# Scores computed in four column tiles, and an order that keeps to one tiling of TensorE

## The chip, the core and the metric

The kernel runs on one core of a Trainium2 chip, as one program in one launch. The metric is the device time of one execution in microseconds (us); lower is better. The times given are medians over several executions. Of the engines, TensorE (PE; its weight loads are shown apart as PEld) does the matrix products, ScalarE (ACT) the exponentials, VectorE (DVE) and GpSimd (POOL) the elementwise work, and SyncE (SP) issues most transfers.

## The reference

Two rounds of two layers, each added to a residual stream of 2048 tokens by 512 features. Layer A is full attention with 32 query heads of 16 features and one head of keys and values. Layer B is attention within four segments of 512 tokens, with a memory that grows from segment to segment. Everything is float32.

```python
def _A_ref(x, wq, wk, wv, wo):
    q = (x @ wq) as [32 heads, 2048, 16];  k = x @ wk;  v = x @ wv
    p = softmax(q @ k.T * 16 ** -0.5)
    return (p @ v, heads side by side) @ wo

def _B_ref(x, wq, wk, wv, wo, beta):          # per head, L = 512
    for s in range(4):
        qs, ks, vs = q[s], k[s], v[s]
        p = softmax(qs @ ks.T * scale + causal mask of the segment)
        a_mem = (phi(qs) @ M) / (phi(qs) @ z + 1e-6)
        o = g * a_mem + (1 - g) * (p @ vs)
        M, z = M + phi(ks).T @ vs, z + sum(phi(ks))
    return o @ wo

x = x + _A_ref(layernorm(x), ...);  x = x + _B_ref(layernorm(x), ...)     # twice
```

## The kernel before

**Two streams.** Work is cut into four blocks of 512 tokens and, for the two rounds, into eight phases f. In phase f the full attention of one block of queries (stream `za`, generator `a_units`) is woven with everything that follows from the block before (stream `zb`, generator `side`): output projection, layer norm, the whole of layer B for that block, its output projection, and the projections that the next full attention needs. Phase 0 weaves the first full attention with the preparation of all keys; after phase 7 the last block's `side` runs alone. Each generator yields, ahead of each piece of work, a function that tells when the piece is ready by the kernel's own account of the engines (`clk`). `weave` takes the next piece from the stream that is ready, and where both are, in proportion to their lengths; `par` does the same among the chains inside one stream. What they choose is the program order, and a scheduler keeps to that on PE apart from small moves. PE runs its instructions in that order.

**A stage of the full attention.** One stage is one tile of 128 keys for 4 heads by 512 queries; there are 1024. It has two score steps (L600), each of two matmuls into a pair of PSUM banks: stationary `kst`, 97 rows (the six products of bfloat16 parts, and a guard row) by 128 keys; moving `qa`, 97 by 512. After each step ACT takes the exponential of the pair, 128 x 1024 (L603), into `pa`. Then `a_pv` multiplies with the values: four float32 matmuls, one for each head, with stationary `va` of 17 columns (16 values and a one for the sum). Each writes 17 partitions of the bank `pva`, from partition 64, 96, 0 and 32, so it occupies 32 columns of the array. `together` records them; the first stands at L77, the other three at L80. A float32 matmul is one instruction in the program's order and two matmul records in the profile, for the two parts of its weights.

**The segment attention.** For each of the 64 units (4 heads of one block) `b_rowmax` computes all scores once for the row maxima (L771; stationary `qb`, moving `kb`, 128 to 512 columns), which DVE reduces (L779). `b_attend` computes them again, transposed (L807), adds the causal mask on the diagonal as a product of the identity `idb` with `maskk` (L810), ACT takes the exponential (L814) and `b_pv` multiplies with the values as `a_pv` does (into `pvb`, with `pb` and `vb`).

**The projections** (`project`, L341) are float32r matmuls at the array's full width, 12 to a result of 128 x 512: four contraction tiles with three products of parts each. They yield after every three. Transposes (L401, L738), the memory (L832, L868) and small products with 32 columns or fewer (L467, L552) are the rest of PE's work.

Of the kernel before, what the change touches and what calls it, by code (L numbers as in the profile page):

```python
# [33 lines left out]
P = 128  # L34
# [33 lines left out]
def net_kernel(ctx, tc, x_in, a_wq, a_wk, a_wv, a_wo, b_wq, b_wk, b_wv, b_wo, b_beta, cst, out):  # L68
# [3 lines left out]
    T = nc.tensor  # L72

    def together(first, *a, **k):
        """a matmul; all but the first of a group follow the one before at once"""
        if first:
            nc.tensor.matmul(*a, **k)  # L77
        else:
            with tc.high_priority(offset=400):
                tc.keep_in_program_order(nc.tensor.matmul(*a, **k))  # L80

# [21 lines left out]
    HOP = 250.0  # from one engine's end to the start of what waits for it on another  # L103
    LOAD = 2600.0  # a small transfer
    clk = {"pe": 0.0, "act": 0.0, "dve": 0.0, "pool": 0.0}
    evac_on = ["dve"]

    def pe(cost):
        clk["pe"] += cost
        return clk["pe"]  # L110
# [41 lines left out]
    # static tiles  # L152
# [32 lines left out]
    def wload(kind, i, w=None, parts=""):  # L185
        """into w, else into the next of the ring; parts: keep the two parts, or take those kept"""
# [56 lines left out]
    # gate of the memory, one value per partition of the (4 heads x 32) layout, column (p, t)  # L243
# [14 lines left out]
    class Ring:  # L258
        """slots of PSUM, taken in turn"""
# [16 lines left out]
    def layout(kind):  # L276
        """banks: scores, row maxima, the rest; 6 and 7 hold the products with the values"""
# [9 lines left out]

    def par(*gens):
        """several chains at once: the first that is ready, else the one that is ready soonest"""
        live = []  # L290
        for g in gens:
            if g is not None:
                try:
                    live.append([g, next(g)])
                except StopIteration:
                    pass
        while live:
            yield lambda: min(z[1]() for z in live)
            now = clk["pe"]
            z = next((z for z in live if z[1]() <= now), None) or min(live, key=lambda z: z[1]())  # L300
# [29 lines left out]
    xr = [0.0] * 4  # when each quarter of xh, xl is there  # L330

    def project(out_, lhs_h, lhs_l, rhs_h, rhs_l, need):
        """out_ = sum over 4 contraction tiles of (h + l)(h + l), without l*l; takes a slot of the ring"""
# [5 lines left out]
        for kt in range(4):  # L339
# [3 lines left out]
            end = pe(648)  # L343
            if kt < 3:
# [5 lines left out]
    def project_t(w):  # L350
        """transposed: [128 columns of w, 512 tokens]"""
# [3 lines left out]
    def slot(shape, need):  # L355
        """a slot of the ring for a short piece of work"""
# [13 lines left out]
    def norm_stats(xt, tiles, t0):  # L370
        """mean and 1/sqrt(var + eps) of token tiles xt (their numbers: tiles), there at t0"""
# [41 lines left out]
    def evac(ps, e):  # L413
        """one reader of a PSUM slot; the rest goes on from SBUF"""
# [7 lines left out]
    def split3(x, t):  # L422
        """three bfloat16 parts that add up to x, there at t"""
# [627 lines left out]
```

## Time and profile before

| | |
|---|---|
| median of 3 runs | 3380.35 us (3379.74 to 3380.38) |
| profiled execution | span 3373.7 us from the first to the last instruction, 6.6 us around it: 3380.3 us |
| busy share of the span | PE 98%, ACT 71%, DVE 49%, PEld 37%, POOL 11% |
| chain that ended last | PE 80%, issue 8%, DVE 5%, DMA 4% |
| score matmuls of the full attention, L600 | 4096, mean 381 ns |
| exponentials of the full attention, L603 | 2048, mean 1022 ns |
| value products, L77 and L80, full attention | 2048 and 6144 records, mean 598 ns |
| granted TensorE clock | 0.990 |

A record's length holds the way through the array, so matmuls that stream one behind the other overlap in the profile; how fast they run is read from the distance between starts. "Issue" in the chain is time in which an engine waited for nothing that the profile shows. Idle time of an engine that is not the bottleneck costs nothing.

### The profile page before, as it was taken

How to read it: one execution, taken by the hardware profiler on the slowest of the kernel's cores; microseconds unless marked ns; L12 is line 12 of the kernel's file. 1: busy time of each engine (PE TensorE's matmuls, PEld its weight loads, DVE VectorE, ACT ScalarE, POOL GpSimd, SP SyncE). 2: the span in 40 equal slices, each digit the busy share in tenths (PEclk: the TensorE clock that was granted, in tenths of full speed). 3: DMA queues.
4: the chain of work that ended last, by engine and by line, in shares of the span. 5: the costliest groups of instructions: out<-in, count | busy, mean ns of one | idle time of the engine just before them, and what ended most of it. 6: DMA issues, size and time to landing. Idle time of an engine off the chain costs nothing.

```text
span 3373.7 us, 53649 instructions
## 1 busy us (share of the span) xinstructions
PE 3289.8 (98%) x20586; PEld 1252.0 (37%) x20586; DVE 1644.6 (49%) x4679; ACT 2404.7 (71%) x2575; POOL 377.6 (11%) x540
## 2 busy tenths in 40 slices
PE   7999999999999999999999999999999999999977
PEld 4422333334333443334433333333433334333533
DVE  7701345454553545645455353555455534553466
ACT  3699777866778667786678878677677776778422
POOL 2100110021100220102110020100110002100100
PEclk9999999999999999999999999999999999999978
DMA  4411121122210231202322142321231215221341
GB/s 133 130 33 29 56 84 56 33 78 85 69 54 20 72 91 56 72 15 82 101 64 75 45 123 78 111 61 52 79 85 50 58 39 161 90 65 29 124 121 42
DMA packets 188674, 244.62 MB, mean 73 GB/s; under 512 B 26904, under 2 KB 147576, under 8 KB 188408
## 3 DMA queue, kind: packets, MB, share of 16 engines
q1 hardware_dynamic: 169272, 176.08, 17.7%
q0 software_dynamic: 19136, 65.02, 6.8%
q8 instruction: 164, 2.69, 0.4%
q14 instruction: 102, 0.84, 0.1%
HBM read 168.41 MB, written 72.61 MB: 71 GB/s over the span
## 4 chain that ended last, share of the span: by engine, by line
PE 80%; issue 8%; DVE 5%; DMA 4%; POOL 2%; ACT 1%; SPq 0%; DVEq 0%; POOLq 0%; ACTq 0%
PE bank L77 28%; PE bank L600 24%; PE bank L341 13%; PE bank L771 4%; PE bank L807 4%; PE bank L810 1%; PE bank L80 1%; DMA sb<-parts 1%; PE bank L832 1%; DVE mo L779 1%; DMA wst<-in_B_wq_dram 1%; PE bank L401 1%; POOL w L120 1%; PE bank L868 1%; ACT pa L603 1%
## 5 line engine op out<-in xcount | busy, mean ns | idle before, releaser
L603 ACT ACTIVATE pa<-bank 128x1024 f32<-128x1024 f32 x2048 | 2010.1, 1022 | 610.9 <-PE bank L600 597.2
L600 PE MATMUL bank<-qa,kst 97*128 97x512 bf16 x4096 | 1147.4, 381 | 3.1 <-ACT pa L603 1.8
L80 PE MATMUL bank<-pa,va 128*17 128x512 f32 x6144 | 1072.0, 598 | 0.0
L77 PE MATMUL bank<-pa,va 128*17 128x512 f32 x2048 | 1057.5, 598 | 2.9 <-DVE t L632 1.9
L779 DVE CUSTOM_DVE_ANT_0 mo<-bank,maskq 128x512 bf16<-128x512 f32 (+3 forms) x1024 | 498.7, 487 | 572.7 <-PE bank L771 557.8
L600 PEld LDWEIGHTS <-kst 97*128 97x128 bf16 x4096 | 313.8, 97 | 796.2 <-issue 640.0
L814 ACT ACTIVATE pb<-bank 128x1024 f32<-128x1024 f32 (+2 forms) x384 | 331.6, 881 | 179.8 <-PE bank L810 143.1
L341 PE MATMUL bank<-xh,w 128*128 128x512 f32 x832 | 322.1, 432 | 6.1 <-DVE qmx L471 2.7
L771 PE MATMUL bank<-kb,qb 96*128 96x512 bf16 (+3 forms) x1024 | 251.7, 309 | 26.4 <-DVE m L779 22.9
L341 PE MATMUL bank<-w,xh 128*128 128x512 f32 x752 | 269.8, 437 | 4.7 <-DVE xh L665 2.1
L77 PEld LDWEIGHTS bank<-pa,va 128*17 128x17 f32 x2048 | 117.5, 95 | 406.8 <-issue 325.2
L120 POOL TENSOR_SCALAR w<-wst 128x512 fp32r<-128x512 f32 x160 | 103.8, 649 | 1272.6 <-PE bank L341 1202.0
L807 PE MATMUL bank<-qb,kb 98*128 98x512 bf16 (+3 forms) x1024 | 222.9, 305 | 4.1 <-ACT pb L814 2.8
L632 DVE STREAM_TRANSPOSE t<-bank 128x512 f32<-128x512 f32 x88 | 62.8, 714 | 298.3 <-PE bank L80 297.9
L771 PEld LDWEIGHTS <-qb 96*128 96x128 bf16 x1024 | 87.2, 99 | 302.4 <-issue 247.2
L341 PEld LDWEIGHTS bank<-xh,w 128*128 128x128 f32 x832 | 158.4, 191 | 86.5 <-issue 32.7
L80 PE MATMUL bank<-pb,vb 128*17 128x512 f32 (+3 forms) x1536 | 186.0, 439 | 0.0
L77 PE MATMUL bank<-pb,vb 128*17 128x512 f32 (+3 forms) x512 | 182.6, 439 | 1.0 <-ACT pb L814 0.4
L341 PEld LDWEIGHTS bank<-w,xh 128*128 128x128 f32 x752 | 135.0, 189 | 109.5 <-issue 45.1
L341 PE MATMUL bank<-xl,w 128*128 128x512 f32 x416 | 166.5, 400 | 1.2 <-DVE xl L409 1.2
L208 DVE TENSOR_TENSOR w<-wst,w 128x512 fp32r<-128x512 f32 x160 | 112.0, 700 | 101.0 <-POOL w L120 100.2
L341 PE MATMUL bank<-w,xl 128*128 128x512 f32 x376 | 150.7, 402 | 0.0
(136 smaller groups left out, 2480.5 us busy)
## 6 DMA issues: line engine op xcount, KB each, us to landing
sb<-parts SPq DMA_DIRECT2D x192, 128.0 KB
qa<-sd SPq DMA_DIRECT2D x88, 196.0 KB
sd<-parts SPq DMA_DIRECT2D x96, 128.0 KB
x<-xt SPq DMA_DIRECT2D x48, 256.0 KB
xt<-x SPq DMA_DIRECT2D x48, 256.0 KB
qb<-sb SPq DMA_DIRECT2D x64, 192.0 KB
kb<-sb SPq DMA_DIRECT2D x64, 192.0 KB
qa<-sd SPq DMA_DIRECT2D x88, 128.0 KB
```

The lines of the kernel that those rows point to most:

```text
L77: nc.tensor.matmul(*a, **k)
L80: tc.keep_in_program_order(nc.tensor.matmul(*a, **k))
L120: G.tensor_scalar(o, i, 1.0, 0.0, op0=ALU.mult, op1=ALU.add)
L208: V.tensor_tensor(w[:, 1, :], s, f(w[:, 0, :]), op=ALU.subtract)
L341: T.matmul(ps, lhsT=l_(kt), rhs=r_(kt), start=n == 0, stop=n == 11)
L600: T.matmul(sc[:, i, :], lhsT=L["kst"][0:rows, kt * P:(kt + 1) * P], rhs=q[0:rows, 2 * u + i, :], start=True, stop=True)
L603: A.activation(x, sc, AF.Exp, scale=0.25)
L632: V.transpose(t1.rearrange("p a b -> p (a b)"), pva)
L771: T.matmul(ps[:, o_:o_ + nk], lhsT=q[0:96, j, qt * P:(qt + 1) * P], rhs=k[0:96, j, 0:nk], start=True, stop=True)
L779: V.tensor_tensor_reduce(out=mo[:, 0:nk], in0=ps[:, o_:o_ + nk], in1=maskq[:, 512 - nk:512], op0=ALU.add, op1=ALU.max, scale=1.0, scalar=- ...
L807: T.matmul(sc[:, i, o_:o_ + nq], lhsT=k[0:98, 2 * u + i, kt * P:(kt + 1) * P], rhs=q[0:98, 2 * u + i, kt * P:512], start=True, stop=False)
L814: A.activation(e[:, :, 0:w], sc[:, :, 0:w], AF.Exp, scale=0.25)
```

## The change

Three things change. The constants of PE's account are edited along with them.

**Scores in four column tiles.** `by_columns` replaces each score matmul and each mask matmul. It takes 32 of the 128 stationary columns at a time, in the order 2, 3, 0, 1, and writes 32 partitions of the same PSUM bank: four weight loads and four matmuls where there was one of each, with the same moving operand. This holds for L600, L771, L807 and L810. No result changes.

**An order that knows the tiling.** A yield may carry its form: `Need(at, "cols")` for the scores and value products, "full" for all else. `tiling` keeps the form of the last work, and a change of form is accounted 95 ns. `par` prefers among the ready chains one whose form is at hand. `weave` compares scores: the time at which a stream could start, 190 ns more if the form changes, and 0.03 of the stream's lead over its share.

**Projections in halves.** They yield once, after six matmuls, and no longer after every three.

```diff
+    def by_columns(first, out_, lhsT, rhs, **k):
+        for c in (2, 3, 0, 1):
+            r_ = slice(32 * c, 32 * c + 32)
+            together(first and c == 2, out_[r_], lhsT=lhsT[:, r_], rhs=rhs, **k)
...
-    def pe(cost):
-        clk["pe"] += cost
+    tiling = ["full"]
+    def pe(cost, form="full"):
+        clk["pe"] += cost + (DRAIN if form != tiling[0] else 0.0)
+        tiling[0] = form
         return clk["pe"]
...
+        def pick():
+            ready = [z for z in live if z[1]() <= clk["pe"]]
+            same = [z for z in ready if form_of(z[1]) == tiling[0]]
+            return (same or ready or [min(live, key=lambda z: z[1]())])[0]
...
-            if ra <= now and rb <= now:
-                use = za if da / ta <= db / tb else zb
-            else:
-                use = za if ra <= rb else zb
+            lag = (da / ta - db / tb) * (ta + tb) / 2
+            def score(z, r, ahead):
+                return max(now, r) + (2 * DRAIN if form_of(z[1]) != tiling[0] else 0.0) + LAG * ahead
+            use = za if za[1] and score(za, ra, lag) <= score(zb, rb, -lag) else zb
...
-            end = pe(648)
-            if kt < 3:
+            end = pe(660)
+            if kt == 1:
                 yield lambda: 0.0
...
-                        T.matmul(sc[:, i, :], lhsT=L["kst"][0:rows, kt * P:(kt + 1) * P],
-                                 rhs=q[0:rows, 2 * u + i, :], start=True, stop=True)
+                        by_columns(i == 0, sc[:, i, :], L["kst"][0:rows, kt * P:(kt + 1) * P],
+                                   q[0:rows, 2 * u + i, :], start=True, stop=True)
...
-                T.matmul(ps[:, o_:o_ + nk], lhsT=q[0:96, j, qt * P:(qt + 1) * P], rhs=k[0:96, j, 0:nk],
-                         start=True, stop=True)
+                by_columns(o_ == 0, ps[:, o_:o_ + nk], q[0:96, j, qt * P:(qt + 1) * P], k[0:96, j, 0:nk],
+                           start=True, stop=True)
...
-                        T.matmul(sc[:, i, o_:o_ + P], lhsT=idb, rhs=maskk, start=False, stop=True)
+                        by_columns(False, sc[:, i, o_:o_ + P], idb, maskk, start=False, stop=True)
```

The account also changes: a value product of the full attention from 940 to 848, one of the segment attention loses 85, a triple of a projection goes from 648 to 660. In the changed kernel the first matmul of a group stands at L81, the others at L84, whatever they compute; projections stand at L378.

What that does to PE's order is seen at three places. First, a stage of the full attention with nothing beside it, before (names as in the profile, with numbers; a row is one instruction, or several alike):

```order
L77 MATMUL bank<-pa_2058,va_16_106 17x512
L80 MATMUL bank<-pa_2058,va_16_106 17x512
L80 MATMUL bank<-pa_2054,va_16_106 17x512 x2
L600 LDWEIGHTS kst_14_104
L600 MATMUL bank<-qa_18_112,kst_14_104 128x512
L600 LDWEIGHTS kst_14_104
L600 MATMUL bank<-qa_18_112,kst_14_104 128x512
```

and the same place on PE now, the last matmul of one stage's scores, its value products, and the start of the first group of the next scores:

```order
L84 MATMUL bank<-qa_19_113,kst_14_104 32x512
L81 MATMUL bank<-pa_3210,va_16_106 17x512
L84 MATMUL bank<-pa_3210,va_16_106 17x512
L84 MATMUL bank<-pa_3200,va_16_106 17x512 x2
L81 LDWEIGHTS kst_14_104
L81 MATMUL bank<-qa_19_113,kst_14_104 32x512
L84 LDWEIGHTS kst_14_104
L84 MATMUL bank<-qa_19_113,kst_14_104 32x512
```

Scores that took one load and one matmul of 128 columns now take four of 32, and everything in the stage has outputs of at most 32 partitions.

Second, a projection of layer B (weights `w`, tokens `xh` and `xl`) woven into the full attention on PE, before:

```order
L600 MATMUL bank<-qa_18_112,kst_14_104 128x512
L341 MATMUL bank<-w_2815,xh_139 128x512 x2
L341 MATMUL bank<-w_2815,xl_140 128x512
L600 LDWEIGHTS kst_14_104
L600 MATMUL bank<-qa_18_112,kst_14_104 128x512
L600 LDWEIGHTS kst_14_104
L600 MATMUL bank<-qa_18_112,kst_14_104 128x512
L77 MATMUL bank<-pa_3399,va_16_106 17x512
L80 MATMUL bank<-pa_3399,va_16_106 17x512
L80 MATMUL bank<-pa_3382,va_16_106 17x512 x2
L341 MATMUL bank<-w_2820,xh_139 128x512 x2
L341 MATMUL bank<-w_2820,xl_140 128x512
```

and such a projection on PE now:

```order
L84 MATMUL bank<-qa_19_113,kst_14_104 32x512
L378 MATMUL bank<-w_7584,xh_139 128x512 x2
L378 MATMUL bank<-w_7584,xl_140 128x512
L378 MATMUL bank<-w_7613,xh_139 128x512 x2
L378 MATMUL bank<-w_7613,xl_140 128x512
L378 MATMUL bank<-w_9708,xh_139 128x512 x2
L378 MATMUL bank<-w_9708,xl_140 128x512
L378 MATMUL bank<-w_9713,xh_139 128x512 x2
L378 MATMUL bank<-w_9713,xl_140 128x512
L81 LDWEIGHTS kst_14_104
L81 MATMUL bank<-qa_19_113,kst_14_104 32x512
```

The pieces of three that stood between scores are now twelve in a row. Runs of exactly twelve were 64 before and are 153 now.

Third, the segment attention on PE, a score step with its mask, before:

```order
L807 MATMUL bank<-qb_21_115,kb_24_118 128x512
L807 LDWEIGHTS kb_24_118
L807 MATMUL bank<-qb_21_115,kb_24_118 128x512
L810 LDWEIGHTS idb_94
L810 MATMUL bank<-maskk_96,idb_94 128x128
```

and one of its shortest steps now, from the end of its scores to the start of its masks:

```order
L84 MATMUL bank<-qb_20_114,kb_23_117 32x128
L84 LDWEIGHTS kb_23_117
L84 MATMUL bank<-qb_20_114,kb_23_117 32x128
L84 LDWEIGHTS idb_94
L84 MATMUL bank<-maskk_96,idb_94 32x128
```

Eight instructions of 128 columns stand where two stood. Over the part of the order that is executed, PE has 22,529 instructions before and 65,537 now, 7168 groups of scores and masks both times; neighbours of different form (outputs over 32 partitions, and at most 32) number 2557 before and 709 now; projections are entered 432 times before, 143 of them from work of at most 32 partitions, and 197 times now, 187 of them so. With the full attention alone there stand runs of 97 and 35 stages before, 103 and 32 now. The other engines are given the same work.

More of the change, by code (lines that the diff above doesn't have):

```diff
@@ L104, in net_kernel @@
     LOAD = 2600.0
+    LAG = 0.03
+    DRAIN = 95.0
     clk = {"pe": 0.0, "act": 0.0, "dve": 0.0, "pool": 0.0}
     evac_on = ["dve"]
-    def pe(cost):
-        clk["pe"] += cost
+    tiling = ["full"]
+    def pe(cost, form="full"):
+        clk["pe"] += cost + (DRAIN if form != tiling[0] else 0.0)
+        tiling[0] = form
         return clk["pe"]
@@ L286, in drive, with __init__, __call__, form @@
             clk["pe"] = max(clk["pe"], rdy())
+    class Need:
+        def __init__(self, at, form):
+            self.at, self.form_ = at, form
+        def __call__(self):
+            return self.at()
+        def form(self):
+            return self.form_() if callable(self.form_) else self.form_
+    def form_of(need):
+        return need.form() if isinstance(need, Need) else "full"
     def par(*gens):
@@ L296, in par @@
                     pass
+        def pick():
+            ready = [z for z in live if z[1]() <= clk["pe"]]
+            same = [z for z in ready if form_of(z[1]) == tiling[0]]
+            return (same or ready or [min(live, key=lambda z: z[1]())])[0]
         while live:
-            yield lambda: min(z[1]() for z in live)
-            now = clk["pe"]
-            z = next((z for z in live if z[1]() <= now), None) or min(live, key=lambda z: z[1]())
+            yield Need(lambda: min(z[1]() for z in live), lambda: form_of(pick()[1]))
+            z = pick()
             try:
@@ L582, in a_units @@
             if pend is not None and (gate(f, n, k1) or nxt is None):
-                yield lambda: max(pend[-1], pva_free[0] if pend[1] else 0.0)
+                yield Need(lambda: max(pend[-1], pva_free[0] if pend[1] else 0.0), "cols")
                 a_pv(*pend)
@@ L595, in a_units @@
                 for u in range(2):
-                    yield lambda: max(need, rings["sc"].ready(), L["kr"][kt // 4], gate(f, n, k1))
+                    yield Need(lambda: max(need, rings["sc"].ready(), L["kr"][kt // 4], gate(f, n, k1)), "cols")
                     ring = rings["sc"]
@@ L599, in a_units @@
                     for i in range(2):
-                        T.matmul(sc[:, i, :], lhsT=L["kst"][0:rows, kt * P:(kt + 1) * P],
-                                 rhs=q[0:rows, 2 * u + i, :], start=True, stop=True)
+                        by_columns(i == 0, sc[:, i, :], L["kst"][0:rows, kt * P:(kt + 1) * P],
+                                   q[0:rows, 2 * u + i, :], start=True, stop=True)
                     x = tmp(4, [P, 2, 512], F32, "pa")
                     A.activation(x, sc, AF.Exp, scale=0.25)
-                    ring.free[k] = on("act", pe(432), 904)
+                    ring.free[k] = on("act", pe(432, "cols"), 904)
                     pe_.append(x)
@@ L612, in a_units @@
                 if pend is not None:
-                    yield lambda: max(pend[-1], pva_free[0] if pend[1] else 0.0)
+                    yield Need(lambda: max(pend[-1], pva_free[0] if pend[1] else 0.0), "cols")
                     a_pv(*pend)
                 pend = (L, kt == k0, kt, pe_, (f, b, n, k0, k1), kt == k1 - 1, max(te))
-        yield lambda: max(pend[-1], pva_free[0] if pend[1] else 0.0)
+        yield Need(lambda: max(pend[-1], pva_free[0] if pend[1] else 0.0), "cols")
         a_pv(*pend)
@@ L627, in a_pv @@
                      start=first, stop=last)
-        e = pe(940)
+        e = pe(848, "cols")
         if not last:
@@ L764, in b_rowmax @@
         for job in jobs:
-            yield lambda: max(need, rings["m"].ready())
+            yield Need(lambda: max(need, rings["m"].ready()), "cols")
             ring = rings["m"]
@@ L770, in b_rowmax @@
                 nk = (qt + 1) * P
-                T.matmul(ps[:, o_:o_ + nk], lhsT=q[0:96, j, qt * P:(qt + 1) * P], rhs=k[0:96, j, 0:nk],
-                         start=True, stop=True)
+                by_columns(o_ == 0, ps[:, o_:o_ + nk], q[0:96, j, qt * P:(qt + 1) * P], k[0:96, j, 0:nk],
+                           start=True, stop=True)
                 o_ += nk
-                e = pe(cols(nk))
+                e = pe(cols(nk), "cols")
             o_ = 0
@@ L798, in b_attend @@
             for s_ in range(1 if kt >= 2 else 2):
-                yield lambda: max(gr[n], rings["sc"].ready())
+                yield Need(lambda: max(gr[n], rings["sc"].ready()), "cols")
                 ring = rings["sc"]
@@ L806, in b_attend @@
                     for i in range(2):
-                        T.matmul(sc[:, i, o_:o_ + nq], lhsT=k[0:98, 2 * u + i, kt * P:(kt + 1) * P],
-                                 rhs=q[0:98, 2 * u + i, kt * P:512], start=True, stop=False)
+                        by_columns(i == 0, sc[:, i, o_:o_ + nq], k[0:98, 2 * u + i, kt * P:(kt + 1) * P],
+                                   q[0:98, 2 * u + i, kt * P:512], start=True, stop=False)
                     for i in range(2):
-                        T.matmul(sc[:, i, o_:o_ + P], lhsT=idb, rhs=maskk, start=False, stop=True)
-                    e_ = pe(2 * cols(nq) + 115)
+                        by_columns(False, sc[:, i, o_:o_ + P], idb, maskk, start=False, stop=True)
+                    e_ = pe(2 * cols(nq) + 115, "cols")
                 w = loc[1][1] + nq
@@ L818, in b_attend @@
             if pend is not None:
-                yield lambda: max(pend[4], v_r[0], pvb_free[0] if pend[0] == 0 else 0.0)
+                yield Need(lambda: max(pend[4], v_r[0], pvb_free[0] if pend[0] == 0 else 0.0), "cols")
                 b_pv(t, p, *pend)
             pend = (kt, nq, es, loc, te)
-        yield lambda: pend[4]
+        yield Need(lambda: pend[4], "cols")
         b_pv(t, p, *pend)
@@ L860, in b_pv @@
                      rhs=es[s_][:, i, o_:o_ + nq], start=kt == 0, stop=kt == 3)
-        pe(nq * 4 / 2.4 + 85)
+        pe(nq * 4 / 2.4, "cols")
     def b_memory(b, t, r):
```

## The prediction

> **What bounds the kernel now.** I read the page's first and fourth parts first: which engine is full, and what the chain that ended last is made of.
>
> ```profile
> PE 3289.8 (98%) x20586; PEld 1252.0 (37%) x20586; DVE 1644.6 (49%) x4679; ACT 2404.7 (71%) x2575; POOL 377.6 (11%) x540
> ...
> PE 80%; issue 8%; DVE 5%; DMA 4%; POOL 2%; ACT 1%; SPq 0%; DVEq 0%; POOLq 0%; ACTq 0%
> ```
>
> PE is full and the chain runs through it. The second entry matters here: for 8% of the span, 270 us, the chain waits for nothing that the profile shows. Next the stretches, since an average hides stages (columns: window, busy us and count of PE, PEld, DVE, ACT, POOL, clock, DMA).
>
> ```profile
> 200.00:300.00 100.00, 100.00 (x618) 22.78 (x615) 10.16 (x20) 98.86 (x103) 1.22 (x2) 1.00 0.10 27
> 1000.00:1100.00 100.00, 99.76 (x722) 34.08 (x721) 44.37 (x153) 81.38 (x88) 1.23 (x2) 1.00 0.09 25
> 3200.00:3300.00 100.00, 76.87 (x443) 39.15 (x442) 70.84 (x244) 27.69 (x36) 8.71 (x14) 0.83 0.42 120
> ```
>
> At 200 to 300 us the full attention runs alone, with PE and ACT both full. At 1000 us two streams are woven, PE is full and ACT has a fifth to spare; most of the span is so. After about 3170 us the last block stands alone and PE has holes. The timeline then shows what a busy PE does in one stage of the full attention (start, length, engine, line):
>
> ```profile
> 251.81 0.60 PE L77 MATMUL bank<-pa,va 128*17 128x512 f32 x1
> ...
> 251.82 0.62 PE L80 MATMUL bank<-pa,va 128*17 128x512 f32 x3
> 251.82 0.10 PEld L77 LDWEIGHTS bank<-pa,va 128*17 128x17 f32 x1
> 251.83 0.11 PEld L80 LDWEIGHTS bank<-pa,va 128*17 128x17 f32 x4
> 252.25 0.59 PE L77 MATMUL bank<-pa,va 128*17 128x512 f32 x1
> ...
> 252.80 1.04 PE L600 MATMUL bank<-qa,kst 97*128 97x512 bf16 x4
> ...
> 253.76 0.60 PE L77 MATMUL bank<-pa,va 128*17 128x512 f32 x1
> ```
>
> Four value products of 17 columns start within 0.01 us of each other, each in its own 32 columns of the array, and their second halves follow after 0.44 us: four run in the time of one. From the last halves to the first scores it is 0.55, that is 0.11 more; from four scores (0.22 each) to the next value product it is 0.96 in place of 0.88, that is 0.08 more. Each change between full width and 32-column tiles costs about 0.10 us in which nothing starts. PE's order holds 2557 such changes: 2557 x 0.10 = 256 us, against the chain's 270.
>
> **The change, part by part.** The baseline is the profiled span, 3373.7 us, and 6.6 us around it: 3380.3, at the median (3380.35).
>
> *Changes of tiling.* In the new order I count 709, so 1848 fall away: 1848 x 0.10 = **-185 us** (the chain's 8%, read as 7.5 to 8.5, gives 0.099 to 0.112 each, so -183 to -207).
>
> *Not gained where ACT is full.* Runs of 97 and 35 stages have nothing beside them; now they are 103 and 32. There a stage takes 253.76 - 251.81 = 1.95 us. ACT cannot follow below two exponentials:
>
> ```profile
> 48.84 3.75 ACT L603 ACTIVATE pa<-bank 128x1024 f32<-128x1024 f32 x4
> ```
>
> Four end 3.75 after the first starts, one takes 1.02, so they start every 0.91: a stage cannot go under 1.82. It can win 0.13, not 0.20: 132 x 0.07 = **+9**. The 38 changes saved after the last full-attention stage lie beside PE's holes: **+4**.
>
> *Projections.* They are now given out in halves and stand mostly whole between tiled work. Entered from tiles, the first three matmuls take longer:
>
> ```profile
> 1110.85 0.74 PE L341 MATMUL bank<-w,xh 128*128 128x512 f32 x2
> 1111.42 0.39 PE L341 MATMUL bank<-w,xl 128*128 128x512 f32 x1
> 1111.65 0.63 PE L341 MATMUL bank<-w,xh 128*128 128x512 f32 x2
> 1112.12 0.40 PE L341 MATMUL bank<-w,xl 128*128 128x512 f32 x1
> ```
>
> 0.57 to the third matmul, against 0.47 in the next three: the first weights are not loaded ahead. The order has 143 such entries before and 187 after: 44 x 0.10 = **+5**. Entries from full-width work fall from 289 to 10; I count nothing for them.
>
> *The scores in four tiles.* These are the groups that become four loads and four matmuls each (L771 and L807 have three more forms of 256 each, of 256, 384 and 512 columns):
>
> ```profile
> L600 PE MATMUL bank<-qa,kst 97*128 97x512 bf16 x4096 | 1147.4, 381 | 3.1 <-ACT pa L603 1.8 <-ACT pb L814 0.8 <-DVE qmx L471 0.3
> ...
> L810 PE MATMUL bank<-maskk,idb 128*128 128x128 bf16 x1024 | 140.7, 220 | 0.0
> ...
> L771 PE MATMUL bank<-kb,qb 96*128 96x128 bf16 x256 | 57.2, 223 | 0.0
> ...
> L807 PE MATMUL bank<-qb,kb 98*128 98x128 bf16 x256 | 32.7, 220 | 0.0
> ```
>
> 4096 + 1024 + 1024 + 1024 = 7168 groups; 3 x 7168 = 21,504 more matmuls and as many more loads. No row shows four bf16 tiles at once, so I bound the price of a group. Below: nothing, since the value products stream as fast as one, and their second loads (251.82, 251.83) stand while the first halves run until 252.25, so loads hide behind matmuls in the same columns. Above: 0.10, the projection's unhidden load of 128 columns. The value products are nearest; I take 2 ns of stagger, 7168 x 0.002 = **+14** (0 to 717).
>
> The Trainium skill, "TensorE: Matmul & The Clock Gate", section "The mechanism", says that a weight load overlaps a running matmul only if it goes to another row group. All four tiles use the same rows, so by that rule every load would be paid and the sum would take the 717. The trace does not agree: the second loads stand 0.42 us before the halves that use them, in the same rows.
>
> *Groups of 128 columns* (1024 + 256 + 256 = 1536) stream for only 0.05 us with four loads each. Below nothing, above 0.05 for a load of 128 two-byte columns (half the projection's 0.10): 0 to 77; I take 7 ns, **+10**.
>
> *Issue.* A group needs 8 instructions in place of 2. The quickest rows are these:
>
> ```profile
> 1323.70 0.28 PE L807 MATMUL bank<-qb,kb 98*128 98x128 bf16 x2
> 1323.82 0.28 PE L810 MATMUL bank<-maskk,idb 128*128 128x128 bf16 x2
> 1323.93 0.28 PE L807 MATMUL bank<-qb,kb 98*128 98x128 bf16 x2
> 1324.05 0.28 PE L810 MATMUL bank<-maskk,idb 128*128 128x128 bf16 x2
> ```
>
> Two pairs of load and matmul start every 0.115 us, 28.5 ns an instruction, and that may be streaming alone. At that rate a stage of the full attention, 36 instructions, needs 1.03 us and hides in its 1.7 us. A segment-attention group needs 8 x 28.5 = 228 ns against about 57, 112, 164 and 216 of streaming: 1536 x 0.171 + 512 x (0.116 + 0.064 + 0.012) = 361 us if nothing hides it. Nothing is the lower end: value products and projections beside it bring few instructions and long streams. I take **+10**.
>
> *Waits.* The softmax, evacuations and transfers are unchanged in number. PE is given its score, attention and value work in longer runs of one tiling, and projections go past it. A projection of 12 matmuls holds back the scores queued behind it for some 2.8 us (four times the 0.70 from 1111.42 to 1112.12), and ACT waits for those. ACT's spare fifth covers it; without that, each of the 1024 - 132 = 892 woven stages could fall to ACT's floor, 892 x 0.07 = 62. I take **+5** (0 to 62).
>
> Sum: 3380 - 185 + 9 + 4 + 5 + 14 + 10 + 10 + 5 = 3252 us.
>
> **The rivals.**
>
> *Slower: issue becomes the bound.* If the segment attention's score groups issue at 28.5 ns an instruction and nothing hides it, the sum without the 24 us for stagger and issue is 3228, and 361 make 3589. It turns slower once more than 152 of the 361 (42%) stay unhidden; midway between, 3485. For it: no stretch of this trace asks for that pace beyond a few groups. Against: after an idle wait for a transfer, a load, its matmul and the next load start within 0.03 us, some 15 ns apart:
>
> ```profile
> 2861.58 0.10 PEld L771 LDWEIGHTS <-qb 96*128 96x128 bf16 x1 [1.45 <-DMA qb<-sb]
> 2861.61 0.38 PE L771 MATMUL bank<-kb,qb 96*128 96x512 bf16 x1 [0.56 <-DMA qb<-sb]
> 2861.61 0.31 PEld L600 LDWEIGHTS <-kst 97*128 97x128 bf16 x2
> ```
>
> And the mean asks for less: the order has 22,529 instructions on PE that run, 7168 x 6 = 43,008 come in, and 65,537 in 3250 us are 50 ns each. Chance 0.11.
>
> The Trainium skill, "TensorE: Matmul & The Clock Gate", section "Back-to-back issue gap", gives some 81 ns as the sustained pace of a load and a 128-column matmul. By that the eight would take 324 ns, and this rival would be likelier; the four rows above, 57 ns a pair, do not agree, though they are short.
>
> *Slower: loads are not hidden in tiles.* By half the projection's price, 0.05 a group, 7168 x 0.05 = 358, so 3238 + 358 = 3596; it decides from 142 / 7168 = 20 ns a group. Only an unhidden load speaks for it, and the early second loads against. Chance 0.06.
>
> By the rule of the Trainium skill on row groups, above, the time would end here or beyond; the trace so far disagrees, by the same second loads.
>
> *A smaller gain: waits take it.* PE falls to ACT's floor also where the streams are woven: 3252 + 57 = 3309, and more if the next block's chain of transfers is late too. That chain has room: the last block, alone, takes about 200 us after 3170, a woven one near 400. Chance 0.12, nearly all still faster.
>
> *No change:* only if the tiles of the scores and of the value products do not count as one tiling, and 0.10 stays with each. Chance 0.03.
>
> **How the numbers follow.** The forecast, PE's saved changes less small prices, has 0.68: 3252, with 3200 to 3300 as its own range. Its low end has all four unknown prices at zero (3213) and a change at 0.107. The whole range goes up to 3350, through waits and an issue price of a third of 361; the two slower rivals, 0.17, lie above it. So 3200 to 3350. About 0.2%, 7 us, is what a measurement of this kernel can tell from none: faster 0.80, within it 0.03, slower 0.17.
>
> **What would show it.** PE and PEld: 42,090 records each. The chain's "issue" falls from 8% to 2 or 3%. In a stage, value products follow scores after about 0.22 us, with no hole; four tiles of a score start within some 0.06 us, and a group comes every 0.22. ACT in 200 to 300 us goes up to 108 or 110 exponentials. If groups come every 0.25 or more, loads are paid; if only the segment attention's groups stretch to 0.2 and more at 128 columns, it is issue; if PE shows new idle time ended by ACT, it is the floor.

## The result and the profile after

| | before | after |
|---|---|---|
| median of 4 runs each, same chip | 3380.05 us | 3321.27 us (3319.36 to 3324.97) |
| ratio, 95% interval | | 0.9831 (0.9817 to 0.9845) |
| span of the profiled execution | 3373.7 us | 3323.1 us |

It is faster by 59 us; 128 were forecast. The time lies within the range, far from 3252.

The page of the changed kernel, engines and chain:

```profile
PE 3168.7 (95%) x42090; PEld 1540.5 (46%) x42090; DVE 1650.5 (50%) x4679; ACT 2378.1 (72%) x2575; POOL 383.3 (12%) x540
...
PE 7%; issue 2%; ACT 1%; DVE 1%; DMA 1%; SPq 0%; POOL 0%; DVEq 0%; ACTq 0%; POOLq 0%
```

The count of records is the one forecast. PE was busy for 98% and is for 95%. The chain is followed back over a small part of the span only here, so its 2% of "issue" proves nothing. Two windows of the woven part, in the columns of the prediction:

```profile
1000.00:1100.00 100.00, 96.94 (x1594) 45.91 (x1591) 39.69 (x130) 83.53 (x90) 1.25 (x2) 1.00 0.07 18
1500.00:1600.00 100.00, 96.73 (x925) 46.93 (x917) 54.63 (x115) 62.32 (x68) 21.21 (x28) 1.00 0.26 76
```

Where PE was full to 99.76 in the first of them, 3 us in 100 are now empty, and ACT is still idle for a sixth of the time in one and over a third in the other. The exponentials, the first matmul of each score step, and the first row-max products (busy, mean ns, then the idle time ahead and what ended it):

```profile
L640 ACT ACTIVATE pa<-bank 128x1024 f32<-128x1024 f32 x2048 | 1985.9, 1030 | 521.0 <-PE bank L84 511.0 <-ACT pa L640 0.2
...
L81 PE MATMUL bank<-qa,kst 97*32 97x512 bf16 x2048 | 779.4, 381 | 42.3 <-ACT pa L640 21.8 <-ACT pb L851 10.9 <-DMA qa<-sd 1.8
...
L81 PE MATMUL bank<-kb,qb 96*32 96x512 bf16 (+2 forms) x640 | 217.5, 342 | 30.1 <-DVE m L816 25.8 <-DMA sb<-parts 1.5 <-DVE mrr L592 0.4
```

Ahead of the scores stood 3.1 us of idle time before; now 42.3, of which ACT ended 32.7. Ahead of the row-max products little more shows than before:

```profile
L771 PE MATMUL bank<-kb,qb 96*128 96x512 bf16 (+3 forms) x1024 | 251.7, 309 | 26.4 <-DVE m L779 22.9
```

That is only what shows: a matmul's record lasts 0.38 us, its stream 0.21, so a wait of under 0.17 us lies hidden under the end of the record ahead.

**An account of PE's time.** To see all of it I summed over PE's records the distance between the starts of neighbouring groups (four column tiles that start within 0.06 us are one group), less the streaming of the first (0.417 ns a column, which gives 0.213 us for 512; twice that for the float32 value products). What is left is a gap. At a change of form up to 95 ns of it (into tiles) or 118 (out of them) is called the change; elsewhere up to 25 ns is called small; all above is a wait, put down to the engine whose semaphore the group waits on. The sum and some 20 us at the start make the span. All in us:

| kernel | span | changes | cost of changes | small gaps | waits | of these for ACT, DVE | streaming |
|---|---|---|---|---|---|---|---|
| before | 3373.7 | 2557 | 262 | 63 | 179 | 35, 57 | 2849 |
| after | 3323.1 | 709 | 70 | 95 | 283 | 125, 91 | 2852 |
| column tiles alone (tiles) | 3356.6 | 1097 | 111 | 91 | 280 | 118, 70 | 2854 |
| order alone (order) | 3384.4 | 2591 | 264 | 75 | 172 | 48, 59 | 2850 |
| no charge for a change in the weave (nopref) | 3340.9 | 869 | 87 | 91 | 286 | 125, 81 | 2854 |
| before, cheaper exponentials | 3368.2 | 2555 | 262 | 67 | 167 | 23, 58 | 2848 |
| after, cheaper exponentials | 3265.3 | 705 | 68 | 81 | 234 | 71, 104 | 2858 |
| before, both cuts | 3359.2 | 2549 | 262 | 67 | 158 | 20, 50 | 2848 |
| after, both cuts | 3244.3 | 703 | 68 | 80 | 212 | 78, 75 | 2858 |
| one ring for two slots (shared) | 3359.9 | 583 | 57 | 92 | 335 | 159, 106 | 2855 |
| before, fourth tile | 3371.3 | 2557 | 262 | 64 | 176 | 32, 55 | 2849 |
| after, fourth tile | 3304.5 | 707 | 70 | 91 | 268 | 114, 89 | 2856 |

From before to after: -192 for the changes, +32 for small gaps, +104 for waits, +3 of streaming, -53 in all; the spans differ by 50.6. The gain was made as forecast, and some two thirds of it were lost to waits for ACT (+90) and DVE (+34). Of DVE's, 13 are row-max products that wait for their slot (32 us before, 45 after).

The +32 of small gaps are not a cost of the tiles. In the kernel before, a projection that follows full-width work is recorded like this:

```profile
1116.51 0.61 PE L600 MATMUL bank<-qa,kst 97*128 97x512 bf16 x2
1116.77 0.82 PE L341 MATMUL bank<-w,xh 128*128 128x512 f32 x2
1117.43 0.40 PE L341 MATMUL bank<-w,xl 128*128 128x512 f32 x1
```

The two scores take 0.43 us to stream, yet the first product is recorded 0.26 after the first score; the third product then comes 0.66 later, in place of 0.47. The account books the first as a negative small gap and the second as a wait for no semaphore. By my sum there are 277 such places before, -42 us in small gaps, and 6 after. With each such pair of gaps taken together, small gaps are about 103 us before and 98 after, entries into projections 24 and 19, and other gaps without a semaphore 24 and 42; what makes those last ones was not taken apart. The distances between starts show it directly: the median from one group of scores of 512 columns to the next is 220 ns before and 218 after, between the halves of the value products 441 and 433, between masks 59 and 59.

### The profile page after: what moved, and what is told of

Read it like the earlier page. It is cut to its first block, busy times and chain, and to the rows that moved or that the text cites. A ratio compares the mean times of both kernels' runs of the same rounds, so it can differ in the third digit from the quotient of the medians.

```text
span 3323.1 us, 96782 instructions
## 1 busy us (share of the span) xinstructions
PE 3168.7 (95%) x42090; PEld 1540.5 (46%) x42090; DVE 1650.5 (50%) x4679; ACT 2378.1 (72%) x2575; POOL 383.3 (12%) x540
## 5 line engine op out<-in xcount | busy, mean ns | idle before, releaser
L640 ACT ACTIVATE pa<-bank 128x1024 f32<-128x1024 f32 x2048 | 1985.9, 1030 | 521.0 <-PE bank L84 511.0
L84 PE MATMUL bank<-qa,kst 97*32 97x512 bf16 x14336 | 1172.4, 381 | 0.7 <-DVE qmx L508 0.7
L84 PE MATMUL bank<-pa,va 128*17 128x512 f32 x6144 | 1060.0, 594 | 0.0
L81 PE MATMUL bank<-pa,va 128*17 128x512 f32 x2048 | 1050.6, 594 | 6.5 <-DVE t L669 5.2
L81 PE MATMUL bank<-qa,kst 97*32 97x512 bf16 x2048 | 779.4, 381 | 42.3 <-ACT pa L640 21.8
L84 PEld LDWEIGHTS <-kst 97*32 97x32 bf16 x14336 | 357.9, 95 | 376.1 <-issue 310.7
L81 PEld LDWEIGHTS <-kst 97*32 97x32 bf16 x2048 | 193.9, 95 | 383.9 <-issue 300.4
L378 PE MATMUL bank<-xh,w 128*128 128x512 f32 x832 | 289.9, 410 | 7.6 <-DVE qmx L508 2.9
L81 PEld LDWEIGHTS bank<-pa,va 128*17 128x17 f32 x2048 | 182.9, 97 | 225.3 <-ACT pa L640 50.9
L378 PE MATMUL bank<-w,xh 128*128 128x512 f32 x752 | 247.2, 410 | 7.6 <-DVE xt L712 2.7
L84 PE MATMUL bank<-kb,qb 96*32 96x512 bf16 (+3 forms) x3456 | 253.2, 298 | 0.0
L81 PE MATMUL bank<-kb,qb 96*32 96x512 bf16 (+2 forms) x640 | 217.5, 342 | 30.1 <-DVE m L816 25.8
L84 PE MATMUL bank<-qb,kb 98*32 98x512 bf16 (+3 forms) x3584 | 223.1, 304 | 0.0
L84 PEld LDWEIGHTS bank<-pa,va 128*17 128x17 f32 x6144 | 198.3, 98 | 0.4
L378 PEld LDWEIGHTS bank<-xh,w 128*128 128x128 f32 x832 | 157.5, 190 | 84.9 <-issue 33.3
L81 PE MATMUL bank<-pb,vb 128*17 128x512 f32 (+3 forms) x512 | 180.8, 434 | 2.2 <-ACT pb L851 1.7
L84 PE MATMUL bank<-pb,vb 128*17 128x512 f32 (+3 forms) x1536 | 182.8, 434 | 0.0
```

What stands on the lines that cost most here:

```text
L378: T.matmul(ps, lhsT=l_(kt), rhs=r_(kt), start=n == 0, stop=n == 11)
L640: A.activation(x, sc, AF.Exp, scale=0.25)
```

## The experiments

Two theories stood against each other at first. A: the new order makes the waits, by picking work that is not ready. B: the drains at changes of form were time in which the exponentials and row maxima caught up; without them the next limit is met, in any order. All ratios are to the kernel before on the same chip. The changed kernel itself ran on one chip, where the kernel before took 3380.05 us; on the chips of the experiments it took 3375.8 to 3377.8. So gains over the changed kernel are taken from two ratios, and each is known to some 7 us.

### Each half of the change alone

*tiles*: the kernel before with `by_columns` in place of its score and mask matmuls, its order by the old account.

> The kernel before with the scores in four column tiles and nothing else: the order, the account of costs and the projections in triples stay as they were. PE's order then holds 1097 changes of tiling (2557 before, 709 in the changed kernel). Theory A, the new order makes PE wait (it groups the tiled work, and takes pieces that are not ready yet): without that order the waits stay as before, 1460 changes x 0.10 = 146 us are saved, a dozen is lost to ACT's floor in the stages that stand alone: about 3245 us. Theory B, the waits come with PE's shorter work and would come in any order: some 90 us of them stay, and there are 388 more changes than in the changed kernel: about 3340 to 3360 us.

Measured: 3358.80 us, ratio 0.9949 (0.9932 to 0.9966).

*order*: the changed kernel with full-width scores.

```diff
-        for c in (2, 3, 0, 1):
-            r_ = slice(32 * c, 32 * c + 32)
-            together(first and c == 2, out_[r_], lhsT=lhsT[:, r_], rhs=rhs, **k)
+        together(first, out_, lhsT=lhsT, rhs=rhs, **k)
```

> The changed kernel with its new order, but every score and mask at full width again, so the planner believes in a tiling that is not there: 2591 changes of tiling, as many as before. Theory A: the order alone costs its waits, 50 to 90 us: 3430 to 3470 us. Theory B: PE's work is as long as before, so no waits come in: 3375 to 3395 us.

Measured: 3388.20 us, ratio 1.0033 (1.0020 to 1.0045).

In the old order the tiles alone save 151 us of changes and lose 101 to waits; the new order without tiles has no more waits than before. So the waits come with the shorter PE work, not with the order: B. The chain of *tiles*, which is whole, shows the same (before it had ACT at 1%):

```profile
PE 57%; ACT 16%; issue 14%; DVE 7%; DMA 4%; POOL 2%; SPq 0%; ACTq 0%; DVEq 0%; POOLq 0%
```

### The choice in the weave

*ready*: where one stream is not ready, the one that is ready first is taken, whatever its form.

```diff
-            use = za if za[1] and score(za, ra, lag) <= score(zb, rb, -lag) else zb
+            if ra <= now and rb <= now:
+                use = za if score(za, ra, lag) <= score(zb, rb, -lag) else zb
+            else:
+                use = za if ra <= rb else zb
```

> The changed kernel, but where only one of the two woven streams is ready that one is taken, as before the change; the preference for the tiling at hand and for the stream behind its share decides only between two that are ready. 733 changes of tiling (709 in the changed kernel). Theory A with the choice of pieces that are not ready as its cause: most of the new waits go, 3321 - 60 to 90 + 2 = 3235 to 3265 us. Theory B, or theory A with the grouping of tiled work as the cause: 3310 to 3325 us.

Measured: 3325.67 us, ratio 0.9849 (0.9832 to 0.9865), 0.7 us above B's band; the waits are 282.

*nopref*: `2 * DRAIN` becomes 0 in `score`.

> The changed kernel, but weaving does not charge the 190 ns for a change of tiling when it compares the two streams; the lead over the share still counts, and a piece that is not ready may still be taken. 869 changes of tiling. If the grouping by tiling is what makes PE wait: 160 more changes cost 16 us and the waits shrink by more, about 3270 us. If taking pieces that are not ready is, through the share of the lead: the waits stay, 3320 to 3340 us.

Measured: 3342.15 us, ratio 0.9895 (0.9879 to 0.9912), 2 us above the band for waits that stay. The charge is worth some 22 us, 16 of them by its 160 changes at 0.10; the waits are the same with it and without (283 and 286). Neither the charge nor the choice of pieces that are not ready makes them.

### Cheaper exponentials, cheaper row maxima

*exp384_after* and *exp384_before* take the full attention's exponential over 384 of each bank's 512 columns. The tiles `pa` are four fixed ones there, set to 1.0 at the start. PE's work is untouched, and its order in the trace differs by small moves only (705 changes of tiling for 709):

```diff
-                    x = tmp(4, [P, 2, 512], F32, "pa")
-                    A.activation(x, sc, AF.Exp, scale=0.25)
+                    x = pa[turn[0] % 4]
+                    turn[0] += 1
+                    A.activation(x[:, :, 0:384], sc[:, :, 0:384], AF.Exp, scale=0.25)
```

> The changed kernel, with the exponential of the full attention's scores taken over 384 of each bank's 512 columns (what the second product reads in the other 128 columns is a constant, so that part of the output is left out); TensorE's instructions and their order are the same. Theory B (TensorE's drains used to cover the time in which a score slot waits for ScalarE; without them TensorE waits for ScalarE and VectorE, some 205 us of waits in the woven middle, 117 of them for ScalarE's exponentials): an exponential falls from 1.03 to about 0.8 us, the waits for ScalarE fall to a third or less, time 3200 to 3260. Rival D (the waits are set by the woven order, by VectorE's chains and by entries into projections, and the exponential is only the last of several to arrive): 3295 to 3322.

> The kernel before, with the same cut: exponentials of the full attention over 384 of 512 columns (that part of the output is left out). Theory B: here the drains cover ScalarE, which TensorE awaits for some 27 us in the middle, so that at most these come back: 3350 to 3377. Rival D: 3365 to 3380. If this kernel gained as much as the changed one does (more than 60 us), ScalarE's pace would not be what sets the two apart, and theory B falls.

Measured: after 3270.73 us, ratio 0.9690 (0.9674 to 0.9706), 48 us below the changed kernel; before 3371.98, 0.9984 (0.9975 to 0.9994), 5 us. The exponentials of the changed kernel with the cut, against 1030 ns above:

```profile
L645 ACT ACTIVATE pa<-bank 128x768 f32<-128x768 f32 x2048 | 1584.0, 809 | 807.8 <-PE bank L84 797.7 <-PE bank L504 1.1 <-ACT pa L645 0.6
```

The same 0.22 us less is worth some ten times as much once the drains are gone. B's band for the changed kernel was missed by 11 us: its waits for ACT fell from 125 to 71, not to a third, and part of them passed to DVE (91 to 104).

*max_half_after*: the row maxima over half of the columns.

```diff
-  V.tensor_tensor_reduce(out=mo[:, 0:nk], in0=ps[:, o_:o_ + nk], in1=maskq[:, 512 - nk:512], ...
+  V.tensor_tensor_reduce(out=mo[:, 0:nk // 2], in0=ps[:, o_:o_ + nk // 2], in1=maskq[:, 512 - nk:512 - nk + nk // 2], ...
```

> The changed kernel, with the row maxima of the segment attention taken over half of the columns on VectorE (those of the other half are left out of the maximum, and the exponential's scale there is smaller, so that it stays finite); TensorE's work is the same. Theory B: VectorE's 51 us of waits in the middle are for the one slot of the row maxima; the instruction falls from 0.46 to about 0.3 us, and a half of these waits comes back: 3285 to 3310. Rival: VectorE's waits are taken over by ScalarE's, which end just behind them: 3312 to 3324.

Measured: 3297.10 us, ratio 0.9767 (0.9751 to 0.9784): 22 us, within B's band. The first row-max products of that kernel, against 25.8 above:

```profile
L81 PE MATMUL bank<-kb,qb 96*32 96x512 bf16 (+2 forms) x640 | 217.3, 342 | 15.5 <-DVE m L816 11.8
```

*both_after* and *both_before* make both cuts.

> The changed kernel, with both cuts at once: exponentials of the full attention over 384 of 512 columns, row maxima over half of the columns (those parts of the output are left out). If ScalarE's exponentials and VectorE's row maxima took the missing 69 us between 3252 and 3321, and do so one after the other, the two gains of 51 and 24 us add: 3240 to 3255. If the two wait for the same moments, the second brings little: 3262 to 3275.

> The kernel before with both cuts (those parts of the output are left out). Theory B (the drains covered both engines there): 3355 to 3374, at most 20 us below the kernel before, and the changed kernel with the same cuts is then 110 to 130 us faster than it, the size of the forecast. Rival: row maxima cost here what they cost in the changed kernel: 3345 to 3352.

Measured: after 3246.31 us, 0.9611 (0.9595 to 0.9627); before 3361.04, 0.9956 (0.9939 to 0.9973). The gains add within the noise (48 + 22 = 70, and 74 is measured). With both engines relieved the change is worth 3361.0 - 3246.3 = 115 us, close to the 128 forecast, against 59 without. So the two cuts bring back 56 of the missing 69 us. Most of that is the exponentials: the row maxima alone were not cut before, but what their cut adds to that of the exponentials is some 10 us there and 26 after. The waits do not end with the cuts: for ACT and DVE they still rise, from 70 to 153.

### Is it the rate or the round trip?

*exp_split_after*: two exponentials of one bank each, so that the first bank is done half an exponential earlier, at the price of more time on ACT.

```diff
-                    A.activation(x, sc, AF.Exp, scale=0.25)
+                    for i in range(2):
+                        A.activation(x[:, i, :], sc[:, i, :], AF.Exp, scale=0.25)
```

> The changed kernel, with each exponential over two banks split into two over one bank each: the same elements, 2048 more instructions on ScalarE, and the first bank of a score slot comes free about half an exponential earlier. If the slots' latency sets the waits (theory B1): 3260 to 3310, faster than the changed kernel. If ScalarE's rate sets them (theory B2): the exponentials take some 0.1 us more a pair, and the time rises to 3340 to 3420.

Measured: 3319.56 us, ratio 0.9832 (0.9815 to 0.9848), against 0.9831: no difference, and both expectations missed. Its page:

```profile
PE 3171.4 (96%) x42090; PEld 1568.6 (47%) x42090; DVE 1652.6 (50%) x4679; ACT 2475.1 (75%) x4623; POOL 380.8 (11%) x540
```

ACT is busy for 97 us more (2475.1 for 2378.1) and the time does not rise, so its rate over the whole span is not the limit; nor is the earlier bank a gain that can be seen. Whether the two cancel was not separated.

*shared*: the slots of row maxima and projections become one ring of two, used in turn.

```diff
+        if kind == "ab":
+            rings["m"] = rings["r"] = Ring([one_[4], one_[5]])
+            rings["r"].free = [n] * 2
```

> The changed kernel, in which the slot of the row maxima and the slot of the projections are one ring of two slots, used by both in turn, while the two streams are woven: a second row-max product may start while VectorE still reads the first. 583 changes of form stand in its order for 709. Theory B: the waits for row maxima (23 us) go, 126 changes fewer are worth 13 us, projections may wait for a slot instead: 3285 to 3312. Rival: the waits pass to ScalarE's exponentials: 3312 to 3330.

Measured: 3361.91 us, ratio 0.9963 (0.9949 to 0.9977): 45 us slower than the changed kernel, against every expectation. It has 126 changes fewer (-13 us) and 52 us more of waits, for ACT (+34) and DVE (+15). The planner's order changed with the ring, and which part of that costs the time was not taken apart.

### The planner's account and its pieces

*calibrated* sets the account to the trace:

```diff
-                    ring.free[k] = on("act", pe(432, "cols"), 904)
+                    ring.free[k] = on("act", pe(432, "cols"), 920) + 110
-                ring.free[z] = on("act", e_, 51 + 1.667 * w)
+                ring.free[z] = on("act", e_, 67 + 1.667 * w) + 110
-                e = on("dve", e, 65 + 1.05 * nk)
+                e = on("dve", e, 240 + 1.04 * nk)
```

> The changed kernel, with the planner's account of the waiting engines set to the trace: exponentials 16 ns and 110 ns more until their slot is free, row maxima of 512 columns 772 ns for 603. 729 changes of form in its order for 709. If the waits come from the account (it takes slots for free that are not, and picks a score step or a row maximum too early), TensorE's waits in the middle fall by 30 us or more: 3270 to 3300. If ScalarE's and VectorE's pace beside shorter products sets them in any order (theory B): 3312 to 3330.

*calibrated_counted* also sets the weave's clock to `ra if use is za else rb` in place of `min(ra, rb)`.

> As the run with the calibrated account, and the weave also counts the wait of a step that it picks before it is ready (its clock goes to the picked stream's time, not to the earlier of both). 719 changes of form. Account: 3265 to 3300. Theory B: 3310 to 3330.

*thirds* lets a projection be left after each triple (`if kt < 3` in place of `if kt == 1`).

> The changed kernel, in which a projection may be left after each of its four triples of products, as in the kernel before (now only after the second): 721 changes of form and 206 entries into projections for 709 and 197, so that a projection can cover more of the moments in which the tiled work waits. If finer pieces of projections can fill the waits: 3290 to 3312. Theory B (each such filling costs two changes of 0.1 us, as much as the wait it fills): 3315 to 3330.

Measured: 3321.82 us (0.9834, 0.9817 to 0.9850), 3325.52 (0.9846, 0.9830 to 0.9863) and 3328.82 (0.9855, 0.9838 to 0.9871). Their waits are 281, 282 and 289. None of the three takes them away: with the orders of *ready* and *nopref*, five orders leave between 281 and 289 us.

### One thing that makes ACT late

ACT is idle for over a quarter of the span and PE still waits for it, so something must hold ACT. The timeline of the changed kernel shows it (start, length, engine, line; in brackets the idle time ahead and what ended it):

```profile
1032.68 0.33 PE L81 MATMUL bank<-qb,kb 98*32 98x384 bf16 x1
...
1033.01 0.30 PE L84 MATMUL bank<-maskk,idb 128*32 128x128 bf16 x8
...
1033.57 0.60 PE L84 MATMUL bank<-pb,vb 128*17 128x512 f32 x3
...
1033.98 0.38 PE L81 MATMUL bank<-qa,kst 97*32 97x512 bf16 x1
...
1034.26 0.81 ACT L851 ACTIVATE pb<-bank 128x768 f32<-128x768 f32 x1 [1.30 <-PE bank L84]
1034.97 1.02 ACT L640 ACTIVATE pa<-bank 128x1024 f32<-128x1024 f32 x1
1035.12 0.38 PE L81 MATMUL bank<-qa,kst 97*32 97x512 bf16 x1 [0.52 <-ACT pb L851]
```

The scores and masks of 1032.68 are done at 1033.31. Their exponential starts at 1034.26, 0.95 later, at the end of 1.30 us in which ACT did nothing: it waits for the value products of 1033.57, which end at 1034.17, since they read the tile that it must write. `pb` has three tiles; two hold the step before and one the first half of this step. So a score slot stays taken until 1035.07, and the score step that needs it waits 0.52, though the other slot's scores had been given at 1033.98. Of the 64 fourth exponentials of a unit, 44 start more than 150 ns after both their scores and the exponential ahead are done, 34 us in all (26 of 64 and 26 us before).

*pb4_after* and *pb4_before* give this step a fourth tile:

```diff
-                e = tmp(3, [P, 2, 512], F32, "pb")
+                e = tmp(2, [P, 2, 384 if kt % 2 else 512], F32, "pc" if kt % 2 else "pb")
-        r = tmp(2, [P, 512], F32, "rest")
+        r = tmp(1, [P, 512], F32, "rest")
```

> The changed kernel, with a fourth tile for the segment attention's exponentials: pb holds three, two of the step before and two of this one, so the fourth exponential of a unit cannot start before TensorE has read the first value product's tile; in the changed kernel's trace it starts over 150 ns after its scores and ScalarE are done 44 times in 64, 34 us in all, and all later exponentials stand behind it on ScalarE's queue. (The steps of 384 columns get two tiles of their own; rest, which VectorE alone uses, goes from two to one to make room.) If these stalls of ScalarE reach TensorE: 3285 to 3308. If the slots' round trip and VectorE set the waits without it: 3312 to 3325.

> The kernel before with the same fourth tile: there the stall is 26 us in 26 places. If the drains covered it, as theory B has it: 3368 to 3380. If it reached TensorE there too: 3350 to 3365.

Measured: after 3307.51 us, 0.9799 (0.9782 to 0.9815), 11 us faster than the changed kernel, some 7 either way, and the fastest version that computes the reference; before 3374.23, 0.9992 (0.9982 to 1.0002), no clear difference. Without the drains the stall costs some 11 us; under them it costs 3, which the noise does not tell from none. The waits fall by 15 and by 3. The same place with the fourth tile:

```profile
1031.42 0.33 PE L81 MATMUL bank<-qb,kb 98*32 98x384 bf16 x1
...
1031.75 0.30 PE L84 MATMUL bank<-maskk,idb 128*32 128x128 bf16 x8
...
1032.10 0.81 ACT L851 ACTIVATE pc<-bank 128x768 f32<-128x768 f32 x1 [0.40 <-PE bank L84]
...
1032.72 0.38 PE L81 MATMUL bank<-qa,kst 97*32 97x512 bf16 x1
...
1033.15 0.38 PE L81 MATMUL bank<-qa,kst 97*32 97x512 bf16 x1
```

The exponential starts 0.05 us after the masks end, and the second score step follows the first after 0.43, in place of 1.14. Scores that wait for the segment attention's exponentials fall accordingly (waits of PE: us, times, longest), first the changed kernel, then with the fourth tile:

```profile
PE bank L81 <- ACT pb L851: 18.0, 48, 0.8
```

```profile
PE bank L81 <- ACT pb L851: 5.0, 17, 0.6
...
PE bank L81 <- ACT pc L851: 0.4, 2, 0.2
```

What holds the rest, 114 us of waits for ACT and 89 for DVE, was not taken apart further. No run gave the scores a third slot, or put drains back where they were.

## Why the prediction was wrong in size

**Right: the changes of tiling.** -185 forecast; the account gives -192. The account limits what a change may cost, so the spans are the better witness: between the changed kernel and *nopref* lie 160 changes and 17.8 us, between it and *tiles* 388 and 33.5, 0.11 and 0.09 each, with equal waits.

**Too high: what the tiles themselves cost.** Stagger, groups of 128 columns and issue were +14, +10 and +10; no run shows any of the 34. A group of scores comes 218 ns after the one ahead, for 220 before, a mask 59 for 59, and small gaps fell by some 5 us. A stage of the full attention alone:

```profile
252.02 0.60 PE L81 MATMUL bank<-pa,va 128*17 128x512 f32 x1
...
252.46 0.59 PE L81 MATMUL bank<-pa,va 128*17 128x512 f32 x1
252.46 0.10 PEld L81 LDWEIGHTS <-kst 97*32 97x32 bf16 x1 [0.31 <-issue]
...
252.89 0.38 PE L81 MATMUL bank<-qa,kst 97*32 97x512 bf16 x1
252.89 0.12 PEld L84 LDWEIGHTS <-kst 97*32 97x32 bf16 x4 [0.31 <-issue]
252.89 0.61 PE L84 MATMUL bank<-qa,kst 97*32 97x512 bf16 x7
253.11 0.10 PEld L81 LDWEIGHTS <-kst 97*32 97x32 bf16 x1
253.11 0.33 PEld L84 LDWEIGHTS <-kst 97*32 97x32 bf16 x7
253.32 0.38 PE L81 MATMUL bank<-qa,kst 97*32 97x512 bf16 x1
...
253.85 0.60 PE L81 MATMUL bank<-pa,va 128*17 128x512 f32 x1
```

The drain of 0.11 between value products and scores is gone (252.46 to 252.89 is 0.43). Two groups stand between 252.89 and 253.32, 0.215 each, with their loads beside running matmuls. So both slower rivals fall. The rule of the Trainium skill, "TensorE: Matmul & The Clock Gate", section "The mechanism", by which such loads would be paid, does not hold here. The same section lets the array pull a load ahead also where it goes to a background weight buffer, which would allow what is seen; no run here tells whether that is the reason.

**Right: the floor where the full attention stands alone.** The stage takes 253.85 - 252.02 = 1.83 us, as forecast from ACT's rate, in place of 1.95. With the cheaper exponentials the same stage is bound by PE:

```profile
240.17 0.59 PE L81 MATMUL bank<-pa,va 128*17 128x512 f32 x1
...
241.89 0.59 PE L81 MATMUL bank<-pa,va 128*17 128x512 f32 x1
```

1.72 us: two halves of value products at 0.43 and four groups of scores at 0.215.

**Half right: the entries into projections.** Those from tiles cost 5 us more (13.9 to 18.5), as forecast. Those from full-width work, counted at nothing, gave back 9.

**Wrong: the term "Waits", +5 with an upper end of 62.** Waits for ACT and DVE rose by 124, where this term and the floor together allowed 14. The step that failed is the sentence "ACT's spare fifth covers it". A fifth spare on average says how much work ACT could take, not how soon it answers. In the place shown above, at 1035.12, PE stands still because one answer is late by more than the other score slot covers, and the drains, 262 us spread over the span, had been cover: relieved ACT and DVE give 15 us before and 74 after. The price of a woven stage's fall to ACT's floor, 0.07, was also no upper bound, since single waits of 0.3 us and more make up 166 us of the 283 (77 of 179 before). DVE's single row-max slot had no term at all. That the time is not further from 3252 is luck in part, since the 34 us counted for the tiles did not come. The rival "a smaller gain: waits take it", 3309, named ACT's part of the cause and came within 12 us, with the same luck and nothing for DVE; 0.12 was too little for it.

The Trainium skill, "TensorEngine Tiling (Array Packing)", section "PSUM Bottleneck", says that tiling speeds up TensorE but not the reading of PSUM, which may then bound. The waits for ACT and DVE agree, 92 us before and 216 after, though ACT stays idle for 28% of the span; the prediction did not weigh this rule.

## What to carry to other kernels

When a stall is removed from an engine that is full, ask what caught up during that stall: count the slots between it and its partners and the time of a round trip, not the partners' average share of busy time. A cheap test is to shorten the partner's work in both kernels; here that was worth 5 us before and 48 after. Then look for places where the partner is idle and late at once: a tile too few cost some 11 us after the change, and before it no more than the noise hides.

## What the runs showed of the hardware

Instructions start faster than the 28.5 ns that the prediction read from the quickest rows. In the changed kernel the two mask groups of 1033.01, eight matmuls of 128 columns, start in the 0.11 us up to the next value product, and eight loads with them: the last four of the masks' and the first four of the value products'.

```profile
1032.85 0.28 PEld L84 LDWEIGHTS <-idb 128*32 128x32 bf16 x8
1033.01 0.30 PE L84 MATMUL bank<-maskk,idb 128*32 128x128 bf16 x8
1033.07 0.10 PEld L81 LDWEIGHTS bank<-pb,vb 128*17 128x17 f32 x1
1033.09 0.10 PEld L84 LDWEIGHTS bank<-pb,vb 128*17 128x17 f32 x3
1033.12 0.59 PE L81 MATMUL bank<-pb,vb 128*17 128x512 f32 x1
```

That is 16 starts at 7 ns each in a short burst, and four small tiles with four loads took no longer than one full-width pair did before, 57 ns. How long PE could keep this pace no run shows.
